# One written order for every engine: from units 0 to 8 to all 48 attention units

## The chip, the cores and the metric

The kernel runs on one core of a Trainium2 chip. Its time is the device time of one execution in microseconds; lower is better. The time before is given as the median of three runs.

## The reference

Three parts in a row, all with float32 inputs and outputs.

```python
# attention: q, k, v of [4, 8, 1152, 64]
q_pool = q.reshape(B, H, S // 2, 2, D).mean(axis=3)
scores = scale * np.matmul(q_pool, k.transpose(0, 1, 3, 2))
attn = softmax(scores)
x = matmul(attn, v)                  # heads beside each other: [2304, 512]
# first dense part
h = x @ w_in                         # [2304, 2048]
g = where(h >= 1, h, where(h <= -1, 0, (h + 1) ** 2 / 4))
x = g @ w_out                        # [2304, 512]
# second dense part
h = maximum(maximum(x @ w1, x @ w2), x @ w3)   # [2304, 768]
return h @ w_o2
```

The weights come as 64-bit numbers and are turned into float32 on the chip (`to_f32`).

## The kernel before

**Units.** The attention is cut into 48 units: unit `n` is batch `b = n // 12`, a block `i` of 192 pooled queries (three in a batch) and a pair of heads `p` (four). In each unit `soft` (L398) runs three times (`who` 0, 1, 2: head 0, head 1, and the 64 last queries of both): scores on PE into a tile of three PSUM banks (`sc`, L394), row maximum on DVE (L409), its scaling to the bias `nb` (L411 on DVE or L414 on ACT), exponential on ACT (L416). For batches 1 to 3 the weights are then split into two float16 halves: for `who` 0 and 1 by ACT and DVE into `hl` (L480, L481), which a transposing DMA on SP's queue carries into `pt` (L482); for `who` 2 by transposes on PE (`tr`, L458), and ACT and DVE write `pt` from PSUM (L466, L467). For batch 0 all three go by transposes on PE in float32. The tiles `sc` and `tr` take turns in two buffers of one pool. `shares` (L423) brings the row sums into the shape of `av`, by two transposes on PE (L433, L434) and two copies on ACT into `R`. `av` (L485) multiplies with v, and `rows` (L518) splits a block's result into the two halves `xh`.

**Dense steps.** For each block of 192 rows there are eight steps up (`up_step`, L550: 24 matmuls `ph`, then ACT `t2`, two DVE operations, ACT and DVE for the halves of `g`) and four steps down (`down_step`, L581: 48 matmuls `py`, two ACT operations, a store to `y_d`). `ph`, `py`, `av` and the small sums take turns in two PSUM banks.

**Weights and inputs.** w_in is loaded and converted in eight chunks (`w_in_chunk`, L191), w_out in eight chunks (`w_ou_chunk`, L234): ACT takes the absolute value (L167), DVE works four times (L169 to L175), ACT squares. Five of the eight chunks of w_out go through one raw buffer (`raw_ou`). When all eight are in, `w_ou_last` (L261) takes the largest value over the partitions, with one transpose on PE (`max_ou`, L113), and only then every chunk is scaled into its halves (L256, L258). k, v and q of later batches are loaded, normed, split (POOL at L280, DVE at L282) and, for k and q, transposed by DMA.

**What sets the order.** Each engine takes its instructions in the order in which they stand, and SP's queue issues the DMAs in its own. Inside `tc.manual_schedule(engines=...)` the named engines keep the order in which the program writes them; elsewhere a scheduler places each instruction. Before, PE is in written order over the whole attention, and the others only in `opening()`: the table `OPENING` there names one piece of work a word (`s01` is unit 0, `who` 1; `w`, `o` weight chunks; `u`, `y` dense steps up and down; `k`, `v`, `q` the inputs; `r` `shares`; `a` `av`; `x` `rows`), and each word takes that generator to its next `yield`. It ends with unit 8's work and with every weight chunk. Units 9 to 47 then run in a loop over `ORDER`: `s0` one score stage, `t0` what follows its exponential, `r` and `a1` `shares` and `av` of the unit before, `d` one call of the dense steps, `q` the next q. There PE's order is the written one, and ACT, DVE, POOL and SP go by the scheduler. After the attention (`at.close()`) the second dense part's weights are converted beside what is left of the dense steps, and its matmuls (`p`, L844) run to the end.

Of the kernel before, what the change touches and what calls it, by code (L numbers as in the profile page):

```python
# [19 lines left out]
K1 = (-2, 0, 2)  # L20
V1 = (1, 2, 3)
# [41 lines left out]
def body(ctx: ExitStack, tc: tile.TileContext, q, k, v, w_in, w_out, w1, w2, w3, w_o2, out):  # L63
# [246 lines left out]
    def k_steps(b, p):  # L310
# [30 lines left out]
    def q_steps(b, i, p):  # L341
# [56 lines left out]
    def soft(b, i, p, who):  # L398
# [14 lines left out]
        if not (FIRST(b, i, p) and who in NB_DVE):  # L413
            nc.scalar.activation(out=nb, in_=m, func=AF.Copy, scale=e, bias=PS)  # L414
# [8 lines left out]
    def shares(b, i, p):  # L423
# [8 lines left out]
        rs = R[b, i, p] if not FIRST(b, i, p) else psg.tile([P, 512], F32, tag="g1", name=f"rs{b}_{i}_{p}")  # L432
# [17 lines left out]
    def turned(b, i, p, who, pf):  # L450
        key = f"{b}_{i}_{p}_{who}"
        if who == 2 or WHOLE(b, p):
# [7 lines left out]
            if who == 2 and not FIRST(b, i, p):  # L460
# [17 lines left out]
        pt = new_pt(b, i, p)  # L478
# [103 lines left out]
    def down_step(b, i, m):  # L582
# [42 lines left out]
    events = {}  # L625

    def steps(gen, *counts):
        for c in counts:
            run(gen, c)
            yield  # L630

    for b in range(1, B):
        for p in range(NPAIR):
            t = 3 * (b * NBL * NPAIR - NPAIR + p + 1)
            for gen, at_ in ((steps(k_steps(b, p), 1, 1, -1), K1), (steps(v_steps(b, p), 1, 1, -1), V1)):
                for x in at_:
                    events.setdefault(t + x, []).append(gen)

    def now(t):
        for gen in events.get(t, ()):  # L640
            next(gen)

    behind = {}

    def piece(name):

        kind, num = name[0], name[1:]
        if kind == "q":
            return q_steps(*units[int(num)])
        if kind == "k":  # L650
            return k_steps(0, int(num))
        if kind == "v":
            return v_steps(0, int(num))
# [11 lines left out]
        if kind == "r":  # L665
            return shares(*units[int(num)])
# [278 lines left out]
```

## Time and profile before

| | us |
|---|---|
| median of the three runs | 1227.33 |
| the three runs | 1227.33, 1227.65, 1220.1 |
| the profiled execution, its own time | 1221.76 |
| its span, first to last instruction | 1220.0 |
| TensorE busy in the span | 1067.8 (88%) |
| VectorE busy | 844.4 (69%) |
| ScalarE busy | 743.4 (61%) |
| GpSimd busy | 143.0 (12%) |

The profile shows one execution. PE is TensorE's matmuls, PEld its weight loads, DVE VectorE, ACT ScalarE, POOL GpSimd, SP the queue that issues the DMAs. PEclk is the TensorE clock that was granted, 1.00 for full speed. The cuts between stages below are the starts of the first row maximum (DVE L409) of units 0, 8, 12, 15, 21, 27, 33, 39 and 47, and the first matmul of the second dense part.

### The profile page before, as it was taken

The numbers are of one execution on the slowest core, as the hardware profiler recorded it, in microseconds if no ns is written. First come the engines' busy times: TensorE is split into PE (matmuls) and PEld (weight loads), VectorE is DVE, ScalarE is ACT, GpSimd is POOL, SyncE is SP. The second block draws the span as 40 slices with busy tenths as digits, with TensorE's granted clock in tenths as the row PEclk, the third lists the DMA queues.
The fourth block names the chain that finished last, engine by engine and source line by source line (L and its number), as shares of the span: only waits on it lengthen the run. The fifth ranks groups of instructions, "written<-read, shape, count | busy, mean of one in ns | idle before, by whom it ended". The sixth has DMA issues, their size and how long they took to land. (4 is left out here: it accounts for less than half of the span.)

```text
span 1220.0 us, 26675 instructions
## 1 busy us (share of the span) xinstructions
PE 1067.8 (88%) x11061; PEld 873.8 (72%) x11061; DVE 844.4 (69%) x1431; ACT 743.4 (61%) x1310; POOL 143.0 (12%) x160
## 2 busy tenths in 40 slices
PE   2778827999999888999987999998978999999998
PEld 1556726787888677888776788887967776777774
DVE  5999957678878789887878878776888552422220
ACT  4988847777778667777867777776465311112111
POOL 3211110121101122010112100000301020100000
PEclk9799968999999899999999999999989999999999
DMA  9844332358666678556588655546443220000001
GB/s 303 233 131 151 87 127 53 91 130 165 111 109 111 133 166 192 103 115 109 104 171 178 119 98 98 99 85 157 143 130 126 73 68 18 10 27 18 18 18 45
DMA packets 273755, 134.92 MB, mean 111 GB/s; under 512 B 229088, under 2 KB 256736, under 8 KB 272608
## 3 DMA queue, kind: packets, MB, share of 16 engines
q1 hardware_dynamic: 273632, 133.20, 47.6%
q8 instruction: 87, 1.43, 0.5%
q14 instruction: 36, 0.29, 0.1%
HBM read 62.39 MB, written 9.44 MB: 59 GB/s over the span
## 5 line engine op out<-in xcount | busy, mean ns | idle before, releaser
L844 PE MATMUL p<-yh,wm 128*128 128x288 f16 x1728 | 216.2, 288 | 4.4 <-POOL yh L815 3.4
L409 DVE TENSOR_REDUCE st<-sc 128x1 f32<-128x1152 f32 x144 | 194.5, 1351 | 27.3 <-PE sc L394 26.9
L592 PE MATMUL py<-g,wou 128*128 128x192 f16 x2304 | 200.8, 248 | 13.2 <-ACT g L576 6.3
L567 PE MATMUL ph<-xh,win 128*128 128x192 f16 x2304 | 206.3, 247 | 2.4 <-DVE xf L514 1.6
L844 PEld LDWEIGHTS <-wm 128*128 128x128 f16 x1728 | 169.5, 98 | 50.8 <-issue 5.0
L592 PEld LDWEIGHTS <-wou 128*128 128x128 f16 x2304 | 192.3, 98 | 15.4 <-issue 10.0
L567 PEld LDWEIGHTS <-win 128*128 128x128 f16 x2304 | 191.2, 98 | 12.1 <-issue 10.4
L416 ACT ACTIVATE pf<-sc,st,esc 128x1152 f32<-128x1152 f32 x144 | 188.6, 1310 | 12.6 <-DVE st L411 5.8
L394 PE MATMUL sc<-kst,qst 128*64 128x512 f16 (+3 forms) x1152 | 171.3, 335 | 21.2 <-ACT pf L416 8.8
L394 PEld LDWEIGHTS <-qst 128*64 128x64 f16 (+1 forms) x1152 | 82.2, 106 | 80.7 <-issue 30.9
L458 PE MATMUL tr<-ident,pf 128*128 128x128 f32 x648 | 90.2, 290 | 18.6 <-ACT pf L416 18.3
L852 ACT ACTIVATE h<-mx 128x288 f16<-128x288 f32 x48 | 21.2, 442 | 130.4 <-DVE mx L850 130.4
L481 DVE TENSOR_TENSOR hl<-pf,hl 128x1152 f16<-128x1152 f32 x72 | 97.1, 1349 | 2.7 <-ACT hl L480 2.7
L500 PE MATMUL av<-pt,vhl 128*64 128x192 f16 x1944 | 94.3, 259 | 2.9 <-DMA pt<-hl 2.9
L458 PEld LDWEIGHTS tr<-ident,pf 128*128 128x128 f32 x648 | 76.4, 150 | 28.0 <-ACT pf L416 18.5
L500 PEld LDWEIGHTS <-vhl 128*64 128x64 f16 x1944 | 86.4, 117 | 13.6 <-issue 10.5
L849 DVE TENSOR_TENSOR mx<-p,mx 128x288 f32<-128x288 f32 x48 | 21.9, 455 | 106.0 <-PE p L844 105.5
L480 ACT ACTIVATE hl<-pf 128x1152 f16<-128x1152 f32 x72 | 83.5, 1159 | 0.9
L576 ACT ACTIVATE g<-t,dgs 128x384 f16<-128x384 f32 x96 | 58.6, 613 | 39.3 <-DVE t L574 39.0
L578 DVE SCALAR_TENSOR_TENSOR g<-t,dgs,g 128x384 f16<-128x384 f32 x96 | 66.4, 694 | 19.2 <-ACT g L576 18.8
L467 DVE TENSOR_TENSOR pt<-tr,pt 128x1152 f16<-128x1152 f32 x36 | 48.8, 1356 | 27.8 <-ACT pt L466 27.8
L573 DVE TENSOR_SCALAR t<-t 128x384 f32<-128x384 f32 x96 | 42.6, 444 | 32.5 <-ACT t L571 30.7
(178 smaller groups left out, 1282.8 us busy)
## 6 DMA issues: line engine op xcount, KB each, us to landing
vn<-in_v_dram SPq DMA_DIRECT2D x16, 576.0 KB, 4.0
kn<-in_k_dram SPq DMA_DIRECT2D x16, 576.0 KB, 4.4
raw_m<-in_moe_w_dram SPq DMA_DIRECT2D x12, 768.0 KB, 5.3
raw_in<-in_moe_w_in_dram SPq DMA_DIRECT2D x8, 1024.0 KB, 6.2
qn<-in_q_dram SPq DMA_DIRECT2D x24, 256.0 KB, 3.3
raw_ou<-in_moe_w_out_dram SPq DMA_DIRECT2D x10, 512.0 KB, 4.3
qst<-qst SPq DMA_DIRECT2D x48, 96.0 KB, 2.2
y_d<-ys SPq DMA_DIRECT2D x48, 96.0 KB, 1.8
```

Source lines behind the costliest of these rows:

```text
L394: nc.tensor.matmul(sc[m0:m1, n0:n1], qst[b, i, p][who][:, var, m0:m1], ks[:, h, n0:n1], start=(var == 0), stop=(var == 1))
L409: nc.vector.tensor_reduce(out=m, in_=sc, axis=AX.X, op=ALU.max, negate=True)
L416: nc.scalar.activation(out=pf, in_=sc, func=AF.Exp, bias=nb, scale=e, accum_out=sums[b, i, p][:, who:who + 1])
L458: nc.tensor.transpose(tr[:, c * P:(c + 1) * P], pf[:, c * P:(c + 1) * P], ident)
L480: nc.scalar.activation(out=hl[:, 0], in_=pf, func=AF.Copy)
L481: nc.vector.tensor_tensor(out=hl[:, 1], in0=pf, in1=hl[:, 0], op=ALU.subtract)
L500: nc.tensor.matmul(acc[64 * h:64 * h + 64], vhl[b, p][:, vi, h, c, :], pt[:, h, pi * KT + c, :], start=(c == 0 and e == 0), stop=(c == KT ...
L567: nc.tensor.matmul(ph[:, a], win[:, wi, kt, ff * P:(ff + 1) * P], x[:, xi, kt], start=(kt == 0 and e == 0), stop=(kt == KD - 1 and e == 2))
L576: nc.scalar.activation(out=g[:, 0, fs, :], in_=t2, func=AF.Copy, scale=gs)
L578: nc.vector.scalar_tensor_tensor(out=g[:, 1, fs, :], in0=t2, scalar=gs, in1=g[:, 0, fs, :], op0=ALU.mult, op1=ALU.subtract)
L592: nc.tensor.matmul(py, wou[:, ff // 2, wi, ff % 2, m * P:(m + 1) * P], g[:, gi, ff, :], start=(ff == 0 and e == 0), stop=(ff == NF - 1 and ...
L844: nc.tensor.matmul(ph[:, :NB2], wm[:, wi, i, kt, ff * P:(ff + 1) * P], yh[:, yi, kt, n0:n0 + NB2], start=(kt == 0 and e == 0), stop=(kt == ...
```

## The change

The loop over `ORDER`, the timed events for k and v, and `OPENING` are gone. One table, `ATTENTION`, names 2279 steps, and all five engines run in written order over the whole attention. It holds k, v and q of every batch, the conversion of w_in and w_out, all steps up and the steps down of the first eleven of the twelve blocks; the last block's four steps down stay with the scheduler. Four generators yield once or twice more, so that a step can stand between the ACT and the DVE half of a split (`turned`) and between the ACT operations and the store (`down_step`). The bias `nb` is made on DVE for all 12 units of batch 0 (before: units 0 to 8), and the same units have a PSUM bank of their own for `shares`.

```diff
-ORDER = {True: "s0 r d s1 d t0 a1 q t1 s2 d d t2",
-         False: "s0 t- d d r s1 t0 a1 s2 t1 q d d"}
-FROM = 9
-FIRST = lambda b, i, p: b == 0 and 4 * i + p < FROM
-NB_DVE = (0, 1, 2)
+NB_DVE = ((0, 1, 2), ())
+OWN_BANK = (True, False)
+ATTENTION = """
+w0 q0 w1 q2 v0 w0 v1 v2 q0 w0 v3 k0 q0 k1 w0 w1 q2 q0 w0 w3 w1 q0 q2 v0 w1 v0 v1 v1 q0 w1 w2 q2 q0 v0 v2 q2 w0
...
+EVERY = {mybir.EngineType.PE, mybir.EngineType.Activation, mybir.EngineType.DVE, mybir.EngineType.Pool,
+         mybir.EngineType.SP}
...
-        if FIRST(b, i, p) and who in NB_DVE:
+        if who in NB_DVE[b > 0]:
             nc.vector.tensor_scalar(out=nb, in0=m, scalar1=e, scalar2=PS, op0=ALU.mult, op1=ALU.add)
...
-        rs = R[b, i, p] if not FIRST(b, i, p) else psg.tile([P, 512], F32, tag="g1", name=f"rs{b}_{i}_{p}")
+        rs = R[b, i, p] if not OWN_BANK[b > 0] else psg.tile([P, 512], F32, tag="g1", name=f"rs{b}_{i}_{p}")
...
                 nc.scalar.activation(out=hi, in_=tr, func=AF.Copy)
+                yield
                 nc.vector.tensor_tensor(out=lo, in0=tr, in1=hi, op=ALU.subtract)
...
         nc.scalar.activation(out=hl[:, 0], in_=pf, func=AF.Copy)
+        yield
         nc.vector.tensor_tensor(out=hl[:, 1], in0=pf, in1=hl[:, 0], op=ALU.subtract)
+        yield
+        pt = new_pt(b, i, p)
         nc.sync.dma_start_transpose(out=pt[:, who, :, 0:P], in_=hl.rearrange("p a b -> p (a b)"))
...
         nc.scalar.activation(out=py, in_=py, func=AF.Square, scale=gd, accum_out=y2[:, b, i, m:m + 1])
+        yield
         copy_q.dma_start(out=y_d[b][:, m, i * NB:(i + 1) * NB], in_=ys)
...
-    order = tc.manual_schedule(engines=ORDERED)
-    order.__enter__()
-    with tc.manual_schedule(engines=OTHERS):
-        opening()
...
-    for n, (b, i, p) in list(enumerate(units))[FROM:]:
-        with tc.issue_after(issued["q"]) if n < LEAD else nullcontext():
-            for word in ORDER[WHOLE(b, p)].split():
-                attend(n, word)
...
+    gens = {}
+    with tc.manual_schedule(engines=EVERY):
+        for name in ATTENTION.split():
             if name not in gens:
                 gens[name] = piece(name)
             run(gens[name], 1)
```

**Place one, PE at the largest value of w_out.** Before, PE's row there (`tr0_2_0_2` is the last transpose of unit 8, `max_ou` the transpose that needs all chunks of w_out, `sc0_2_1_0` the first scores of unit 9):

```order
L567 MATMUL ph0_0_6_1621<-xh0_0_996,win_73 128x192
L458 MATMUL tr0_2_0_2_1660<-ident_80,pf0_2_0_2_1651 128x128 x9
L113 MATMUL max_ou_1695<-ident_80,um_ou_1689 128x128
L394 LDWEIGHTS qst0_2_0_1095
L394 MATMUL sc0_2_1_0_1720<-kst0_1_229,qst0_2_0_1095 128x512
```

Now, in the changed kernel (`sc0_2_1_2` is the last scores of unit 9, `av0_2_0` unit 8's product with v):

```order
L472 MATMUL sc0_2_1_2_1871<-kst0_1_245,qst0_2_0_1526 64x128
L191 MATMUL max_ou_1889<-ident_80,um_ou_1837 128x128
L576 MATMUL av0_2_0_1895<-pt_0_2_0_1700,vn0_0_138 64x192 x18
L184 MATMUL sum_k1_1_1925<-sqk1_1_1893,ones_78 128x1
L536 MATMUL tr0_2_1_1_1929<-ident_80,pf0_2_1_1_1922 128x128 x9
```

`max_ou` has moved from ahead of all three score stages of unit 9 to behind them.

**Place two, DVE at the same point.** Before, DVE's row up to the first row maximum of unit 9 (`wou`, `raw_ou` are chunks of w_out, `um_ou` their largest values):

```order
L170 TENSOR_SCALAR wou_74<-wou_74 128x1024
L173 SCALAR_TENSOR_TENSOR wou_74<-raw_ou_708,wou_74 128x1024
L175 SCALAR_TENSOR_TENSOR wou_74<-raw_ou_708,wou_74 128x1024
L169 TENSOR_SCALAR raw_ou_708<-raw_ou_708 128x1024
L170 TENSOR_SCALAR raw_ou_708<-raw_ou_708 128x1024
L173 SCALAR_TENSOR_TENSOR raw_ou_708<-raw_ou_708 128x1024
L175 SCALAR_TENSOR_TENSOR raw_ou_708<-raw_ou_708 128x1024
L265 TENSOR_REDUCE um_ou_1689<-mx_ou_853 128x1
...
L115 TENSOR_REDUCE U_ou_75<-max_ou_1695 128x1
...
L409 TENSOR_REDUCE st0_2_1_0_1730<-sc0_2_1_0_1720 128x1
```

Now (`st0_2_0_2` is unit 8's last row maximum, `st0_2_1_0` and `st0_2_1_1` are unit 9's first two):

```order
L247 TENSOR_SCALAR raw_ou_589<-raw_ou_589 128x1024
L248 TENSOR_SCALAR raw_ou_589<-raw_ou_589 128x1024
L487 TENSOR_REDUCE st0_2_0_2_1760<-sc0_2_0_2_1713 128x1
L489 TENSOR_SCALAR st0_2_0_2_1760<-st0_2_0_2_1760,esc0_2_0_1645 128x1
L251 SCALAR_TENSOR_TENSOR raw_ou_589<-raw_ou_589 128x1024
L253 SCALAR_TENSOR_TENSOR raw_ou_589<-raw_ou_589 128x1024
...
L487 TENSOR_REDUCE st0_2_1_0_1820<-sc0_2_1_0_1763 128x1
...
L343 TENSOR_REDUCE um_ou_1837<-mx_ou_695 128x1
...
L487 TENSOR_REDUCE st0_2_1_1_1884<-sc0_2_1_1_1860 128x1
```

The last two chunks stood in a row before unit 9; now the last chunk stands among unit 8's work, the one before it further ahead, and the largest value is taken inside unit 9.

**Place three, PE in a regular unit (42).** Before, what stands between the transposes of unit 41's last stage and the second scores of unit 42 (`ph3_0_2` is one step up, 24 pairs of a weight load and a matmul):

```order
L458 MATMUL tr3_1_1_2_10464<-ident_80,pf3_1_1_2_10342 128x128 x9
L567 LDWEIGHTS win_73
L567 MATMUL ph3_0_2_10476<-xh3_0_10075,win_73 128x192
...
L433 MATMUL tr3_1_1_2_10464<-ident_80,rb3_1_1_10509 128x128
L434 MATMUL tr3_1_1_2_10464<-ident_80,sm3_1_1_10193 128x128
L394 LDWEIGHTS qst3_1_2_10361
L394 MATMUL sc3_1_2_1_10516<-kst3_2_8600,qst3_1_2_10361 128x512
```

Now:

```order
L536 MATMUL tr3_1_1_2_10473<-ident_80,pf3_1_1_2_10451 128x128 x9
L648 LDWEIGHTS win_73
L648 MATMUL ph3_0_2_10490<-xh3_0_10195,win_73 128x192
...
L648 MATMUL ph3_0_3_10522<-xh3_0_10195,win_73 128x192
...
```

Behind the first step up now stands a second one (`ph3_0_3`), which before stood behind the third scores; the two transposes of `shares` stand behind the second scores.

## Rows read from the trace of the kernel before

**Rows 1.** Busy time by stage: us, busy (instructions) per engine, PEclk, DMA share, GB/s

```profile
0.00:30.60 30.60, 7.68 (x24) 4.37 (x24) 17.19 (x43) 14.50 (x23) 9.65 (x13) 1.00 0.98 303
30.60:148.90 118.30, 95.28 (x820) 72.38 (x822) 113.30 (x205) 103.91 (x152) 17.39 (x18) 0.93 0.53 150
148.90:255.10 106.20, 73.29 (x722) 61.30 (x723) 69.35 (x122) 68.95 (x113) 14.88 (x18) 0.86 0.35 94
255.10:304.00 48.90, 44.57 (x535) 38.46 (x536) 42.62 (x78) 37.45 (x71) 8.66 (x10) 1.00 0.77 157
304.00:396.90 92.90, 88.56 (x1116) 77.34 (x1115) 74.93 (x111) 72.66 (x134) 9.24 (x14) 1.00 0.63 110
396.90:506.90 110.00, 94.84 (x1125) 81.96 (x1124) 91.45 (x155) 79.02 (x146) 20.18 (x21) 0.95 0.74 156
...
599.70:710.10 110.40, 95.01 (x1126) 81.37 (x1124) 91.46 (x155) 78.76 (x146) 19.49 (x21) 0.95 0.73 146
710.10:833.50 123.40, 117.62 (x1483) 102.66 (x1482) 94.39 (x133) 93.75 (x170) 5.80 (x11) 1.00 0.53 94
833.50:929.90 96.40, 78.10 (x918) 74.78 (x917) 77.38 (x125) 57.62 (x93) 12.80 (x6) 0.93 0.45 138
929.90:1220.00 290.10, 284.38 (x2096) 201.92 (x2095) 97.38 (x206) 63.94 (x130) 15.75 (x15) 0.99 0.12 39
```

**Rows 2.** Timeline, 149 to 200 us: start, us, engine, line, operation, idle before

```profile
169.07 1.12 ACT L167 ACTIVATE wou<-raw_ou 128x1024 f32<-128x1024 f32 x1 [2.29 <-DMA raw_ou<-in_moe_w_out_dram]
170.23 0.69 DVE L169 TENSOR_SCALAR wou<-wou 128x1024 f32<-128x1024 f32 x1 [2.79 <-ACT wou L167]
...
173.69 1.22 DVE L175 SCALAR_TENSOR_TENSOR wou<-raw_ou,wou 128x1024 uint32<-128x1024 uint32 x1
...
179.81 1.12 ACT L167 ACTIVATE raw_ou<-raw_ou 128x1024 f32<-128x1024 f32 x1 [3.65 <-DMA raw_ou<-in_moe_w_out_dram]
...
186.77 0.48 PE L113 MATMUL max_ou<-ident,um_ou 128*128 128x128 f32 x1 [22.55 <-DVE um_ou L100]
```

**Rows 3.** Timeline of unit 42, 756 to 771 us

```profile
756.15 1.15 PE L458 MATMUL tr<-ident,pf 128*128 128x128 f32 x9
...
757.14 2.14 PE L567 MATMUL ph<-xh,win 128*128 128x192 f16 x24
757.34 1.13 ACT L466 ACTIVATE pt<-tr 128x1152 f16<-128x1152 f32 x1 [1.14 <-PE tr L458]
...
758.50 1.36 DVE L467 TENSOR_TENSOR pt<-tr,pt 128x1152 f16<-128x1152 f32 x1 [0.79 <-ACT pt L466]
758.74 1.31 ACT L416 ACTIVATE pf<-sc,st,esc 128x1152 f32<-128x1152 f32 x1
...
760.00 0.30 PE L433 MATMUL tr<-ident,rb 128*128 128x128 f32 x1 [0.72 <-DVE pt L467]
...
760.25 1.14 PE L394 MATMUL sc<-kst,qst 128*128 128x512 f16 x6
...
760.65 0.36 DVE L573 TENSOR_SCALAR t<-t 128x384 f32<-128x384 f32 x1 [0.79 <-ACT t L571]
761.04 0.56 DVE L574 SCALAR_TENSOR_TENSOR t<-t 128x384 f32<-128x384 f32 x1
...
761.32 2.42 PE L500 MATMUL av<-pt,vhl 128*64 128x192 f16 x54
...
764.05 0.61 DVE L578 SCALAR_TENSOR_TENSOR g<-t,dgs,g 128x384 f16<-128x384 f32 x1
764.16 6.05 SPq L482 DMA_TRANSPOSE pt<-hl  x2
...
766.63 4.12 PE L592 MATMUL py<-g,wou 128*128 128x192 f16 x48
```

**Rows 4.** Timeline, 25 to 29 us: POOL and DVE beside each other

```profile
25.54 2.05 POOL L280 TENSOR_SCALAR kpre<-kn,sb 128x1152 f16<-128x1152 f32 x1 [1.16 <-issue]
...
26.54 2.13 DVE L175 SCALAR_TENSOR_TENSOR wou<-raw_in,wou 128x1024 uint32<-128x1024 uint32 x1
```

More of the change, by code (lines that the diff above doesn't have):

```diff
@@ L1 @@
-from contextlib import ExitStack, nullcontext
+from contextlib import ExitStack
 import concourse.bass as bass
@@ L459, in turned @@
             yield
-            if who == 2 and not FIRST(b, i, p):
+            if who == 2 and not OWN_BANK[b > 0]:
                 R[b, i, p] = rs
@@ L639, in now @@
[L639 to L643, printed above, removed]
     def piece(name):
         kind, num = name[0], name[1:]
[L648 to L653, printed above, removed]
-        if kind == "w":
-            return w_in_last() if num == "i" else w_in_chunk(int(num))
-        if kind == "o":
-            return w_ou_last() if num == "o" else w_ou_chunk(int(num))
-        if kind in "uy":
-            i, m = int(num[0]), int(num[1])
-            begun.add((kind, 0, i, m))
-            return (up_step if kind == "u" else down_step)(0, i, m)
-        if kind == "s":
-            n, who = int(num[:-1]), int(num[-1])
-            return soft(*units[n], who)
-        if kind == "r":
-            return shares(*units[int(num)])
-        if kind == "a":
-            return av(*units[int(num)])
-        if kind == "x":
-            return rows(0, int(num))
@@ L672, in opening @@
-    def opening():
-        gens = {}
-        for name in OPENING.split():
+        if name == "wi":
+            return w_in_last()
+        if name == "oo":
+            return w_ou_last()
+        if kind in "suy":
+            n, m = (int(x) for x in num.split("."))
+            if kind == "s":
+                return soft(*units[n], m)
+            begun.add((kind, *divmod(n, NBL), m))
+            return (up_step if kind == "u" else down_step)(*divmod(n, NBL), m)
+        n = int(num)
+        if kind in "kv":
+            return (k_steps if kind == "k" else v_steps)(*divmod(n, NPAIR))
@@ L676, in opening @@
+        if kind in "wo":
+            return (w_in_chunk if kind == "w" else w_ou_chunk)(n)
+        if kind == "x":
+            return rows(*divmod(n, NBL))
+        return {"q": q_steps, "r": shares, "a": av}[kind](*units[n])
+    gens = {}
+    with tc.manual_schedule(engines=EVERY):
+        for name in ATTENTION.split():
             if name not in gens:
@@ L678, in opening @@
             run(gens[name], 1)
-        for name in gens:
-            run(gens[name])
-    order = tc.manual_schedule(engines=ORDERED)
-    order.__enter__()
-    with tc.manual_schedule(engines=OTHERS):
-        opening()
-    for t in range(3 * FROM):
-        now(t)
-    def attend(n, word):
-        b, i, p = units[n]
-        kind, num = word[0], word[1:]
-        if kind == "s":
-            who = int(num)
-            behind[n, who] = soft(b, i, p, who)
-            run(behind[n, who], 3)
-            now(3 * n + who)
-        elif kind == "t":
-            key = (n - 1, 2) if num == "-" else (n, int(num))
-            if key in behind:
-                run(behind.pop(key))
-        elif kind == "r":
-            run(shares(*units[n - 1]))
-        elif kind == "a":
-            attended(n - int(num))
-        elif kind == "d":
-            next(dense, None)
-        elif kind == "q":
-            if n % 2 == 1 and n + 1 < len(units):
-                run(q_steps(*units[n + 1]))
-    def attended(n):
-        b, i, p = units[n]
-        run(av(b, i, p))
-        if p == NPAIR - 1:
-            run(rows(b, i))
-    for n, (b, i, p) in list(enumerate(units))[FROM:]:
-        with tc.issue_after(issued["q"]) if n < LEAD else nullcontext():
-            for word in ORDER[WHOLE(b, p)].split():
-                attend(n, word)
-    last = len(units)
-    run(behind.pop((last - 1, 2)))
-    run(shares(*units[last - 1]))
-    for n in range(last - DEPTH, last):
-        attended(n)
-    order.__exit__(None, None, None)
+    for gen in gens.values():
+        assert next(gen, "end") == "end"
     at.close()
```

141 lines of the change are left out of this document (103 added, 38 removed).

## The prediction

> **What bounds the kernel now.** I read busy time by stage first, cut at the first row maximum of chosen units, then the timeline where a stage was too long, then a regular unit. [rows 1] shows five kinds of stage. From 30.6 to 148.9 us (units 0 to 7) DVE is busy 113.3 of 118.3: there the written order of all engines already stands, and the busiest engine is 96% full. From 148.9 to 255.1 (units 8 to 11) no engine reaches 73.3 of 106.2. The regular stages take 92.9 us for six units and 123.4 for eight, 15.43 a unit, with PE busy 117.62 of 123.4. The two long ones at 396.9 and 599.7 take 110 for six units, where k and v of the next batch are prepared: PE 94.84, DVE 91.45. The tail from 833.5 to 929.9 has PE at 78.1 and DVE at 77.38 of 96.4. From 929.9 PE is busy 284.38 of 290.1, and nothing there is changed: I carry 290.1 over.
>
> In the slow stage the rows to see are [rows 2]: PE stands 22.55 us before `max_ou`. It is next in PE's row, and needs the last chunk of w_out. The chunks come one by one through one raw buffer: from one chunk's first ACT operation (169.07) to the next one's (179.81) is 10.74 us, while DVE works some 4 us on each (two operations of 0.69 and two of 1.22). All engines stand on this chain, with unit 9 ready behind it.
>
> In a regular unit [rows 3] PE runs the transposes `tr`, one step up (757.14 and 2.14 long, so to about 759.2), and then stands until 760.00 for DVE's `pt`; the second scores start at 760.25, and the exponential that frees their buffer ends at 758.74 + 1.31 = 760.05. That is PE's idle time of (123.4 - 117.62) / 8 = 0.72 us a unit.
>
> **The change, stage by stage.** The sum goes by the profiled execution: 1221.76, of which 1220.0 is its span, 1.8 around it.
>
> *Start.* SP now loads two chunks of w_in (128 x 2048 words of four bytes, 1.05 MB each) and one more q (0.39 MB) ahead of the first k: 2.5 MB, at the 303 GB/s of [rows 1] 8.2 us later. DVE has 10 us more to do ahead of the first row maximum (two chunks more at 3.8, and the halves of two at 1.3), but can begin earlier. Bounds 0 and +11; I take +6: 36.6.
>
> *Units 0 to 7.* DVE's work is the same to within 1 us, and was 96% full. Four chunks of w_out now lie in units 5 to 8, each with about 10.5 us of DVE work from one to the next, just under the chain's 10.74. I add 0.75 for each: 118.3 + 3 = 121.3. Bounds: 113 (DVE alone) and 140 (if each chunk cost 5 us).
>
> *Units 8 to 11.* Two chunk conversions go ahead of unit 8; steps up fall from 9 to 2 in matmuls, from 9 to 3 and 4 in their DVE work; steps down from 3 to 1. DVE, by [rows 2, 3]: 69.35 - 6 x (0.36 + 0.56) - 5 x 0.61 - 2 x 3.8, less one split of k and two of q (2.6), plus nine biases moved from ACT (1.9): 52. ACT falls by the same pieces, 68.95 to about 55. PE: 73.29 - 7 x 2.14 - 2 x 4.12 = 50. `max_ou` now stands behind unit 9's three score stages, and the largest value is taken inside that unit, so the 22.55 has unit 9 and k of batch 1 as cover; if that cover is late, it comes back. With ACT at 55 and DVE at 52, both well filled but neither alone, I take 90% of the busier: 62. Bounds 55 and 85 (106.2 less the work that left DVE, if no wait goes).
>
> *Regular units* (15 to 20, 27 to 32, 39 to 46: 20). Two steps up now stand between `tr` and the second scores: 4.2 us of PE work from 757.14, against 2.9 until the exponential ends and 2.7 until `pt` is written. DVE now does a `g` half and sometimes a q split ahead of `pt`, 1.2 us, and the transposes that wait for it stand behind the second scores, so there is room. Late next is nothing: ACT has 93.75 / 8 = 11.7 and DVE 11.8 a unit. Between 0 and 0.72 I take 0.57, as some gaps are the pipeline's own: 14.86 a unit. Stages: 92.9 - 3.4 = 89.5; 92.8 (506.9 to 599.7) - 3.4 = 89.4; 123.4 - 4.6 = 118.8.
>
> *Units 12 to 14.* Equal work, PE busy 44.57 of 48.9: I take 46, between the two.
>
> *Long stages* (21 to 26, 33 to 38). What was put off is made up here: two steps up and one down in each, 2 x 2.14 + 4.12 = 8.4 us of PE work, 3.1 of DVE. PE 94.84 + 8.4 = 103.2, DVE 94.5. Lower bound 103, upper 110 + 8.4 = 118.4 (if the extra work is simply added). Written order held DVE at 96% in the opening, so I take PE at 97%: 106 and 106.4.
>
> *Tail.* Ahead of unit 47 as many dense steps are done as before (84 up, 38 down). Behind the last `av` stand 8 up and 8 down, before 10 and 9: 2 x 2.14 + 4.12 = 8.4 us less on PE, moved into unit 47. DVE's work is unchanged at 77. The scheduler still places the conversion of the last weights. I take 92, between 88 (all of it) and 97.
>
> Sum: 36.6 + 121.3 + 62 + (46 + 89.5 + 106 + 89.4 + 106.4 + 118.8) + 92 + 290.1 = 1158.1; with 1.8 around it 1159.9. The median of the three runs is 5.6 above the profiled one, and one of the three 1.7 below it; I add 2 and say 1162.
>
> **The rivals.**
>
> *The put-off work is only late (no better pace behind unit 12).* For it: PE's row in a regular unit hardly differs, and 95% is already high. Against: the 0.72 has a named cause that the new row removes. From 255.1 to 833.5 are 578.4 us; with the 16.8 us of dense work added, 595.2 instead of 556.1: 1201.
>
> *The chain of chunks stays the bound.* Five chunks through one buffer cost at least 10.74 each whatever the order. If DVE's work between them doesn't fit and each of the four in units 5 to 8 costs 5 us more: +20, 1182. For it: all engines now wait in written order, so one late chunk holds them all. Against: 10.5 beside 10.74.
>
> *POOL and DVE hold each other up.* [rows 4] shows DVE's L175 at 2.13 us beside a POOL operation of 2.05; alone it took 1.22 [rows 2]. If in the long stages every POOL microsecond stops DVE, they cannot be shorter than 94.5 + 20.18 = 114.7: +17 on both, 1179. Against: 91.45 already holds the collisions of before. The Trainium skill, SBUF — State Buffer, section "SBUF: two separate sides", says why: the port pair that the two share is an exclusive lock, held for a whole instruction, so that the other is blocked. The row agrees for this one pair of operations.
>
> *SP's written queue comes late, and the kernel is slower.* Place: the two transposing DMAs of each unit of batches 1 to 3 (36 units). They take 6.05 us to issue [rows 3], now in fixed order with the loads of q, k and v; `av` waits for them. Laid out with the durations of [rows 3] (an estimate), the second `hl` is ready some 14.3 us into a unit, and `av` starts 7.5 into the next, 8 us later. One issue takes 3, landing some 2 more, so about 3.4 are spare. Lateness beyond 3.4 costs PE one for one. At 6 us late: 36 x 2.6 = 94, so 1256. It decides the sign from about 5.2 us (36 x 1.8 = 65, all of the gain). Against: the regular stages of before show no such wait at `av`, with DMA share 0.53 to 0.63.
>
> *Everything fits.* Start and units 0 to 7 lose nothing (-9), units 8 to 11 take 56, the long stages 103, the tail 88: -25, 1137.
>
> **Chances.** Forecast 0.50, no better pace 0.17, chunks 0.11, ports 0.07, SP's queue 0.05, everything fits 0.10. The range 1136 to 1203 takes in all but the slower case and some of the edges. The forecast alone: 1148 to 1174. A measurement of this kernel can tell about 1% from no change: faster by more 0.89, within 0.05, slower 0.06.
>
> **What would show it.** Right: PE's wait before `max_ou` under 5 us; unit 12's first row maximum near 220; 14.9 us from unit to unit in regular stages, with no PE wait on the exponential; the long stages at 106 with PE over 100 busy; the second dense part's first matmul near 868. Wrong: regular units still at 15.4; `av` waiting for `pt<-hl`; unit 8 later than 165; a tail of 97 or more, which would mean that the last weights' conversion bounds it, and not PE.

## The result, and the profile after

The changed kernel takes 1155.88 us (median of four, 1153.67 to 1159.74), the kernel before in the same comparison 1226.52: a ratio of 0.944, 95% interval 0.940 to 0.948. Its profiled execution took 1153.67, with a span of 1151.9 against 1220.0.

Busy time by stage of the changed kernel, with the columns of [rows 1]; the cuts are again the first row maximum (now DVE L487) of units 0, 8, 12, 15, 21, 27, 33, 39 and 47 and the first matmul of the second dense part (now L854):

```profile
0.00:39.80 39.80, 7.67 (x24) 4.45 (x24) 29.81 (x57) 21.22 (x32) 11.48 (x14) 1.00 1.00 314
39.80:163.30 123.50, 100.79 (x892) 77.62 (x892) 115.75 (x202) 102.59 (x151) 18.41 (x19) 0.93 0.52 139
163.30:223.90 60.60, 51.20 (x439) 39.01 (x439) 51.99 (x93) 49.35 (x76) 10.74 (x10) 0.89 0.32 83
223.90:272.30 48.40, 45.46 (x504) 38.39 (x503) 42.85 (x68) 39.43 (x72) 11.71 (x11) 1.00 0.72 154
272.30:361.90 89.60, 89.60 (x1167) 79.33 (x1164) 79.33 (x124) 72.86 (x134) 10.45 (x15) 1.00 0.70 130
361.90:462.10 100.20, 98.50 (x1232) 87.52 (x1231) 90.24 (x152) 82.50 (x156) 22.36 (x21) 1.00 0.87 172
462.10:548.80 86.70, 86.70 (x1111) 76.63 (x1109) 76.20 (x119) 72.43 (x135) 9.85 (x14) 1.00 0.63 118
548.80:653.90 105.10, 99.14 (x1220) 87.59 (x1218) 91.00 (x153) 82.46 (x155) 20.62 (x21) 0.98 0.79 154
653.90:770.00 116.10, 116.10 (x1483) 102.63 (x1482) 98.53 (x155) 93.80 (x174) 7.49 (x15) 1.00 0.60 105
770.00:862.90 92.90, 78.19 (x919) 75.22 (x918) 77.45 (x123) 55.54 (x87) 11.09 (x6) 0.91 0.49 146
862.90:1151.90 289.00, 282.95 (x2096) 201.56 (x2095) 98.27 (x208) 65.68 (x137) 15.27 (x15) 1.00 0.12 40
```

Read it against [rows 1] by PE's idle time, the stage less PE's busy time. Over the span it fell from 152.2 to 95.6, and PE's busy time from 1067.8 to 1056.3; together these are the 68.1 us. The idle time went in units 8 to 11 (32.9 to 9.4), in the two long stages (15.2 to 1.7 and 15.4 to 6.0) and in the regular units (39 to 46: 5.8 to 0). It grew in the start, 22.9 to 32.1, and is about as before in units 0 to 7, 23.0 to 22.7. One count in the table misleads: one `av` (50 of its 54 matmuls, 2.2 us) now falls behind the cut at 272.3, so units 15 to 20 hold 51 matmuls more than before (1167 against 1116), and units 12 to 14 lack them.

A regular unit of the changed kernel (42), PE alone; it answers to [rows 3]. No row has an idle time in brackets, and from one `tr` to the next are 14.5 us:

```profile
697.21 1.15 PE L536 MATMUL tr<-ident,pf 128*128 128x128 f32 x9
698.20 4.12 PE L648 MATMUL ph<-xh,win 128*128 128x192 f16 x48
702.16 1.14 PE L472 MATMUL sc<-kst,qst 128*128 128x512 f16 x6
703.14 0.28 PE L511 MATMUL tr<-ident,rb 128*128 128x128 f32 x1
...
711.72 0.50 PE L536 MATMUL tr<-ident,pf 128*128 128x128 f32 x3
```

At the largest value of w_out, where [rows 2] show 22.55 us, PE now comes straight from unit 9's scores:

```profile
181.31 1.17 PE L472 MATMUL sc<-kst,qst 128*64 128x512 f16 x12 [0.24 <-ACT pt L551]
182.41 0.32 PE L191 MATMUL max_ou<-ident,um_ou 128*128 128x128 f32 x1
182.66 3.15 PE L576 MATMUL av<-pt,vn 128*64 128x192 f32 x36
```

### The profile page after: what moved, and what is told of

It is laid out like the page before. It is cut to its first block, busy times and chain, and to the rows that moved or that the text cites. A ratio compares the mean times of both kernels' runs of the same rounds, so it can differ in the third digit from the quotient of the medians.

```text
span 1151.9 us, 26593 instructions
## 1 busy us (share of the span) xinstructions
PE 1056.3 (92%) x11061; PEld 870.0 (76%) x11061; DVE 851.4 (74%) x1440; ACT 737.9 (64%) x1301; POOL 149.5 (13%) x160
## 4 chain that ended last, share of the span: by engine, by line
PE 44%; DVE 3%; DMA 1%; ACT 1%; issue 1%; SPq 0%; POOL 0%; ACTq 0%; POOLq 0%; DVEq 0%
PE p L854 18%; PE py L673 7%; PE ph L648 6%; PE po L871 5%; PE sc L472 3%; PE av L581 3%; PE tr L536 1%; PE por L885 1%; DVE t L654 1%; DMA vn<-in_v_dram 0%; DVE st_m L247 0%; DMA raw_o<-in_moe_w_out_dram 0%; DVE st_m L253 0%; DVE st_m L251 0%; DMA kn<-in_k_dram 0%
## 5 line engine op out<-in xcount | busy, mean ns | idle before, releaser
L648 PE MATMUL ph<-xh,win 128*128 128x192 f16 x2304 | 209.0, 251 | 9.7 <-POOL xh L358 7.1
L854 PE MATMUL p<-yh,wm 128*128 128x288 f16 x1728 | 214.8, 286 | 1.6 <-DVE yh L827 0.8
L487 DVE TENSOR_REDUCE st<-sc 128x1 f32<-128x1152 f32 x144 | 194.7, 1352 | 20.9 <-PE sc L472 20.3
L648 PEld LDWEIGHTS <-win 128*128 128x128 f16 x2304 | 197.8, 100 | 14.3 <-issue 9.9
L854 PEld LDWEIGHTS <-wm 128*128 128x128 f16 x1728 | 169.0, 98 | 47.0 <-issue 2.5
L673 PEld LDWEIGHTS <-wou 128*128 128x128 f16 x2304 | 189.7, 98 | 13.8 <-issue 12.7
L859 DVE TENSOR_TENSOR mx<-p,mx 128x288 f32<-128x288 f32 x48 | 21.8, 456 | 105.1 <-PE p L854 104.6
L581 PE MATMUL av<-pt,vhl 128*64 128x192 f16 x1944 | 87.1, 247 | 0.0
L581 PEld LDWEIGHTS <-vhl 128*64 128x64 f16 x1944 | 79.3, 110 | 6.8 <-issue 6.4
L652 ACT ACTIVATE t<-ph,Uv 128x384 f32<-128x384 f32 x96 | 55.0, 574 | 15.7 <-PE ph L648 14.7
L871 PE MATMUL po<-wo,h 128*128 128x512 f16 x288 | 64.3, 379 | 0.0
L659 DVE SCALAR_TENSOR_TENSOR g<-t,dgs,g 128x384 f16<-128x384 f32 x96 | 62.0, 648 | 2.7 <-ACT g L657 2.4
```

The lines of the kernel that those rows point to most:

```text
L487: nc.vector.tensor_reduce(out=m, in_=sc, axis=AX.X, op=ALU.max, negate=True)
L581: nc.tensor.matmul(acc[64 * h:64 * h + 64], vhl[b, p][:, vi, h, c, :], pt[:, h, pi * KT + c, :], start=(c == 0 and e == 0), stop=(c == KT ...
L648: nc.tensor.matmul(ph[:, a], win[:, wi, kt, ff * P:(ff + 1) * P], x[:, xi, kt], start=(kt == 0 and e == 0), stop=(kt == KD - 1 and e == 2))
L659: nc.vector.scalar_tensor_tensor(out=g[:, 1, fs, :], in0=t2, scalar=gs, in1=g[:, 0, fs, :], op0=ALU.mult, op1=ALU.subtract)
L673: nc.tensor.matmul(py, wou[:, ff // 2, wi, ff % 2, m * P:(m + 1) * P], g[:, gi, ff, :], start=(ff == 0 and e == 0), stop=(ff == NF - 1 and ...
L854: nc.tensor.matmul(ph[:, :NB2], wm[:, wi, i, kt, ff * P:(ff + 1) * P], yh[:, yi, kt, n0:n0 + NB2], start=(kt == 0 and e == 0), stop=(kt == ...
```

## The experiments

Stage times below are one profiled execution of each kernel, cut as above. The same stage of kernels that share its order differs by up to 2.7 us from one profile to the next (units 0 to 7: 122.7 to 125.3; units 33 to 38: 104.5 to 107.2), and no less is read as a difference unless a wait shows it. Line numbers in some of these kernels are three lower than in the changed one.

### PE's row alone

`e1_phase` is the kernel before with one call of the dense steps more in unit 15. One turn in four is empty, so from there on each `d` of `ORDER` meets another step:

```diff
         for word in ORDER[WHOLE(b, p)].split():
...
+            if n == 15:
+                next(dense, None)
```

> The kernel before with one more turn of the dense steps consumed in unit 15, so that PE's row of a regular unit becomes: first scores, tr, step up, step up, shares, second scores, as in the changed kernel; the other engines stay with the scheduler. Theory A (PE's row alone removes the idle time of 0.72 us a unit): a regular unit takes 14.5 to 14.9 us instead of 15.4, the 20 regular units together 11 to 18 us less, the median 1208 to 1216. Rival B (the gain needs all engines in written order, or comes from work put off): a regular unit stays within 0.15 of 15.4 and the median within 4 us of before.

Measured: 1187.74 against 1224.41, ratio 0.970 (0.968 to 0.973). Its stages of units 15 to 20, 21 to 26 and 39 to 46:

```profile
308.30:395.50 87.20, 87.20 (x1112) 77.03 (x1111) 72.61 (x106) 69.40 (x131) 7.53 (x12) 1.00 0.61 110
395.50:499.50 104.00, 93.33 (x1128) 82.26 (x1127) 88.99 (x158) 79.07 (x150) 19.66 (x23) 0.97 0.82 167
...
691.50:808.20 116.70, 116.14 (x1483) 102.70 (x1481) 94.10 (x133) 91.03 (x170) 5.08 (x12) 1.00 0.61 99
```

Theory A holds for the regular units: they take 14.5 to 14.7 us with the other four engines still under the scheduler, and all 20 together 16.9 less, inside the 11 to 18 expected. The whole gain, 36.7 us, is over twice that. I had left out that the long stages have the same place in their units: they fell from 110 to 104, 12.6 together, without any written order of DVE, and the tail by 4.4. (The profiled execution is the slowest of its four, so the two profiles differ by 29.7 and not by 36.7.)

`e2_back` undoes the same thing in the changed kernel: the five words of the second step up of units 39 to 46 go back behind the third scores (here `u9.1` in unit 41; its first word is PE's, and `s41.1` and `s41.2` are the second and third scores):

```diff
-... s41.0 s40.2 u9.1 u9.0 r40 u8.7 u9.0 r40 s41.1 s41.0 u8.7 r40 a40 s41.1 u9.0 r40 u9.1 s41.0 s41.1 s41.2 a40 ...
+... s41.0 s40.2 u9.0 r40 u9.0 r40 s41.1 s41.0 r40 a40 s41.1 u9.0 r40 s41.0 s41.1 s41.2 u9.1 a40 ...
```

> The changed kernel with the second step up of units 39 to 46 moved back behind the third scores, all else in its written order. Theory A (what stands between tr and the second scores sets a regular unit): units 39 to 46 go from 14.5 to 15.2 to 15.4 us each, the stage from 116.1 to 121 to 124, with PE waiting for DVE's pt or the exponential. Rival B (the written order of the other engines gives the pace): 14.5 to 14.7 each, the stage at 116 to 118.

The eight units take 127.1 us (659.9 to 787.0), 15.9 each, above theory A's 15.4. PE waits again ahead of the second scores, now for the exponential (ACT L491), 7.6 us in seven waits over the stage; here one of them:

```profile
722.84 1.15 PE L533 MATMUL tr<-ident,pf 128*128 128x128 f32 x9
723.83 2.14 PE L645 MATMUL ph<-xh,win 128*128 128x192 f16 x24
726.89 1.14 PE L469 MATMUL sc<-kst,qst 128*128 128x512 f16 x6 [0.92 <-ACT pf L491]
```

The two runs show the cause from both sides: two steps up between `tr` and the second scores cover DVE's `pt` and the exponential, one doesn't. In the whole kernel the 1176.64 (one run) is 20.8 above the changed one; of that 11.0 lie in these units. The rest, 2.7 of it in the tail, lies in stages whose order is the same, and is not explained.

### Units 8 to 11: cover, put-off work, or the other engines' order

Five kernels take this stage apart. `e3_unit9` writes unit 9's score stages ahead of the largest value in `OPENING` of the kernel before (`FROM` becomes 10, which also gives unit 9 its bias on DVE and its `shares` a bank of their own; the four dense turns of unit 9 are made up in units 10 and 11):

```diff
-... o5 o6 s82 u06 s82 u06 u06 o6 o6 o6 o7 o6 o7 o7 o7 o7 oo oo oo ...
+... o5 o6 s82 u06 q10 s82 u06 u06 s90 r8 s91 s90 r8 o6 s91 r8 s90 q10 o6 s91 r8 s90 a8 o6 q10 s91 s92 s90
+a8 q10 o7 s91 q10 s92 o6 q10 s92 o7 q10 s92 o7 s92 q10 o7 o7 oo oo oo ...
```

> The kernel before with the three score stages of unit 9, and shares and av of unit 8 and the next q, put ahead of the largest value of w_out in the written table; the two stretches of scheduled units behind are unchanged. Theory A (the 22.55 us lacked cover): PE's wait before max_ou falls below 8 us and the median by 15 to 20, to 1207 to 1212. Rival B (the gain of units 8 to 11 in the changed kernel comes from dense steps and inputs put off, or the chunk chain bounds anyway): the wait or its like stays, the median within 8 us of before.

`e3c_put_off` takes the dense turns out of units 9 to 11 of the kernel before (`if n >= 12:` ahead of `next(dense, None)`), and `e3b_both` does both.

> The kernel before with the twelve turns of dense steps of units 9 to 11 put off to later units and nothing else: unit 9 still stands behind the largest value of w_out. Theory A (both are needed): PE's wait before max_ou stays at 18 to 24 us and unit 12's first row maximum at 241 to 255. Rival B (putting off alone is the gain of these units): unit 12 at 225 to 237.

> The kernel before with unit 9's score stages ahead of the largest value of w_out (as in the run e3_unit9) and, beside it, the twelve turns of dense steps of units 9 to 11 put off to later units; DVE, ACT, POOL and SP stay with the scheduler from unit 10 on. Theory A (cover and put-off dense steps are needed together, and no written order of the other engines): no wait at max_ou or for the scaled chunks of w_out above 6 us, units 8 to 11 take 76 to 88 us, unit 12's first row maximum at 225 to 237 (before 255.1, changed kernel 223.9). Rival B (the other engines' written order is what is needed): unit 12 stays behind 245.

`e7_pe_only` is the changed kernel with PE alone in written order from `s9.0` on:

```diff
-    with tc.manual_schedule(engines=EVERY):
-        for name in ATTENTION.split():
+    cut = names.index("s9.0")
+    with tc.manual_schedule(engines={mybir.EngineType.PE}):
+        with tc.manual_schedule(engines=EVERY - {mybir.EngineType.PE}):
+            written(names[:cut])
+        written(names[cut:])
```

> The changed kernel with the whole table as PE's order, but from unit 9's first scores on ScalarE, VectorE, GpSimd and SP go by the scheduler, as before. Theory A (PE's row carries the gain behind unit 14, the written order of the others and of SP's loads carries that of units 9 to 11): regular units at 14.5 to 14.7 us, the two long stages 100 to 106, but units 8 to 11 take 70 us or more (60.6 in the changed kernel), so that unit 12's first row maximum is at 233 or later; in all 8 to 25 us slower than the changed kernel. Rival B (PE's row is all of it): unit 12 within 4 us of 223.9, the time within 5 us of 1155.9. Rival C (the others' written order is needed everywhere): regular units at 15.2 or more.

`e9_no_cover` is the changed kernel with the eight words `s9.0 s9.0 s9.0 s9.0 s9.1 s9.0 s9.2 s9.1` moved from ahead of the last `oo` to behind it.

> The changed kernel with the eight steps of unit 9 that stand ahead of the largest value of w_out moved behind it, on all engines. Theory A (these steps are the cover of the wait): PE waits 8 to 16 us before max_ou instead of not at all, and unit 12's first row maximum comes 6 to 14 us later, at 230 to 238. Rival B (the last chunks came early enough by themselves): the wait stays below 4 us and unit 12 within 3 us of 223.9.

| kernel | units 8 to 11 | PE busy there | wait at `max_ou` | unit 12 starts | time, us |
|---|---|---|---|---|---|
| before | 106.2 | 73.29 | 22.55 | 255.1 | 1226.52 |
| `e3c_put_off` | 99.0 | 55.19 | 23.53 | 250.4 | 1231.43 |
| `e3_unit9` | 119.1 | 82.97 | 4.98 | 268.2 | 1229.39 |
| `e3b_both` | 93.3 | 55.62 | 4.63 | 241.4 | 1224.69 |
| `e7_pe_only` | 70.8 | 52.40 | none | 234.1 | 1186.71 |
| `e9_no_cover` | 70.3 | 53.74 | 1.88 | 234.5 | 1166.97 |
| changed | 60.6 | 51.20 | none | 223.9 | 1155.88 |

The times are medians; those of the kernels from `e3c_put_off` to `e9_no_cover`, `e3_unit9` apart, are of one run each. The times of `e3c_put_off` and `e3b_both` don't price the stage, since their put-off turns are made up in the tail, which grows from 96.4 to 110.2 and 112.1. The ratio of `e3_unit9` (ten runs) is 1.005 (1.003 to 1.007), half a per cent slower. This kernel took the wait away as theory A said, and the time came back at once. (Its 82.97 us of PE are for 724 matmuls, before 722, at a granted clock of 0.81 and not 0.86.) PE's row there has a step down close behind `max_ou`, and its matmuls wait chunk by chunk for the scaled w_out; then the second k of batch 1 is late:

```profile
190.01 0.47 PE L113 MATMUL max_ou<-ident,um_ou 128*128 128x128 f32 x1 [4.98 <-DVE um_ou L100]
...
204.98 0.34 PE L592 MATMUL py<-g,wou 128*128 128x192 f16 x2 [1.10 <-ACT wou L256]
206.84 0.50 PE L592 MATMUL py<-g,wou 128*128 128x192 f16 x4 [1.51 <-DVE wou L258]
...
236.85 0.59 PE L106 MATMUL sum_k<-sqk,ones 128*128 128x1 f32 x2 [10.44 <-ACT kpre L297]
```

With the dense turns put off as well the waits for scaled chunks are gone, but the late k stays, in `e3b_both`:

```profile
187.48 0.47 PE L113 MATMUL max_ou<-ident,um_ou 128*128 128x128 f32 x1 [4.63 <-DVE um_ou L100]
...
220.25 0.59 PE L106 MATMUL sum_k<-sqk,ones 128*128 128x1 f32 x2 [13.00 <-ACT kpre L297]
```

So 241.4 lies between theory A's 237 and rival B's 245, and neither stands as put. Putting work off alone left the 22.55 in place (23.53), as theory A said. In the changed kernel the table loads both k's ahead of unit 8 and keeps `y0.0` behind unit 11's scores; the early k's were not tried by themselves. `e7_pe_only` keeps that PE row and takes away the others' written order from unit 9 on: 10.2 us come back here. `e9_no_cover` returns 9.7, with unit 12 at 234.5 as expected, but not as a long wait at `max_ou`, as I had put it; from unit 8's first row maximum to unit 9's are 24.9 us instead of 12.2, and PE's idle time in the stage grows from 9.4 to 16.6 in several waits.

`e7_pe_only` also splits the whole gain. Its span is 1184.8, so 35.2 of the 68.1 us are there with PE's row and the written part up to unit 8; 32.9 need the other engines' order. Its stages of units 8 to 11, 15 to 20, 21 to 26, 33 to 38 and 39 to 46:

```profile
163.30:234.10 70.80, 52.40 (x446) 39.09 (x444) 51.47 (x103) 52.39 (x82) 14.29 (x15) 0.88 0.38 93
287.10:377.10 90.00, 89.82 (x1167) 79.38 (x1166) 75.11 (x113) 70.56 (x135) 8.90 (x14) 1.00 0.62 114
377.10:489.30 112.20, 101.46 (x1235) 89.77 (x1233) 91.97 (x164) 82.12 (x156) 19.09 (x22) 0.98 0.75 156
575.40:687.40 112.00, 100.35 (x1226) 87.96 (x1225) 95.10 (x164) 81.46 (x157) 22.90 (x22) 0.98 0.72 145
687.40:803.10 115.70, 115.70 (x1479) 102.23 (x1478) 94.02 (x134) 91.28 (x172) 5.31 (x12) 1.00 0.60 101
```

The regular units need PE's row alone. The long stages don't: with the dense work made up in them they take 112 under the scheduler and 100.2 and 105.1 in written order. I had expected 100 to 106 there, and the time is 30.8 above the changed kernel's, not 8 to 25.

### The start

`e4_start` puts the first words, up to `s2.0`, back into the order of `OPENING`.

> The changed kernel with its first steps, up to the first scores of unit 2, in the order of the kernel before (k ahead of most of w_in), the rest in its own order. Theory A (the later first row maximum is only VectorE work done early): unit 0's first row maximum goes back from 39.8 to about 31, and that of unit 8 stays within 3 us of 163.3. Rival B (the later first unit is time lost): unit 8's comes 5 to 9 us earlier, at 154 to 158, and the end with it.

```profile
0.00:31.10 31.10, 7.68 (x24) 4.38 (x24) 17.20 (x43) 14.40 (x23) 9.80 (x13) 1.00 0.98 300
31.10:168.80 137.70, 101.58 (x885) 79.23 (x886) 126.12 (x215) 109.64 (x158) 19.84 (x20) 0.91 0.52 148
```

Unit 0 starts at 31.1 again, and unit 8 not earlier but 5.5 us later, at 168.8: theory A's 3 us are missed too, and rival B falls. The whole run takes 1157.89 (one run). From the kernel before to the changed one, unit 8 is later by the DVE work done ahead of it: DVE is busy 130.5 of 148.9 before and 145.6 of 163.3 in the changed kernel, so that 18.4 and 17.7 are left idle. In `e4_start` almost the same work, 143.3, leaves 25.5 idle. The lateness is there by unit 2, whose first row maximum comes at 75.0 and not at 69.1, with DVE idle for 18.8 us up to there against 10.7; from unit 2 to unit 8 the two are alike (93.8 and 94.2). So the late first unit is not time lost: DVE does work there that it otherwise does later, with more idle time.

### What is left: the tail and a late v

Two edits tried the tail, where PE still idles 14.7 us. `e5_tail` moves `y10.0` and `y10.1` ahead of `u11.0` on PE, `e6_no_pool` takes GpSimd out of the split of w1 to w3:

```diff
-... a47 r47 y9.3 a47 x11 x11 x11 u11.0 u11.1 ...
+... a47 y10.0 r47 y9.3 a47 y10.1 y10.0 x11 x11 x11 y10.0 y10.1 u11.0 u11.1 ...
```

```diff
-            if kt == 0:
-                nc.scalar.activation(out=wm[:, 0, :, kt, :], in_=st, func=AF.Copy, scale=s[:, kt:kt + 1])
-                nc.gpsimd.tensor_scalar(...)
-                nc.gpsimd.tensor_tensor(...)
-            else:
-                split_rows(...)
+            split_rows(...)
```

> The changed kernel with two of the last-but-one block's steps down (8.2 us of PE work) moved in PE's row ahead of the last block's steps up, into the 7.1 and 1.4 us in which PE waits for xh behind the last av. Theory A (the tail is bound by PE's row): the tail from unit 47's first row maximum to the second dense part's first matmul goes from 92.9 to 85 to 89 us, the median from 1155.9 to 1148 to 1152. Rival B (the tail is bound by the conversion of the last weights on VectorE and ScalarE): the tail stays within 2 us of 92.9.

> The changed kernel with the split of the first of the four blocks of w1 to w3 done as the other three are (ScalarE, then one VectorE operation) and not on GpSimd. In the changed kernel a VectorE operation that alone takes 0.35 us took 4.69 beside GpSimd's 4.73 and one of 0.56 took 2.47, and TensorE then waited 5.73. Theory A (GpSimd's two operations stop VectorE): VectorE does 2 to 2.6 us more but loses 6 less, TensorE's wait of 5.73 falls below 2.5, the tail of 92.9 falls by 2 to 5 us. Rival B (the tail hangs on the loads or on ScalarE, and the stop is hidden): the tail within 1.5 us of 92.9 or longer.

The changed kernel's tail, all engines, shows why both were worth a run:

```profile
802.04 0.32 PE L648 MATMUL ph<-xh,win 128*128 128x192 f16 x1 [7.10 <-POOL xh L358]
...
812.67 4.73 POOL L775 TENSOR_TENSOR wm<-st_m,wm 128x2304 f16<-128x2304 f32 x1
812.92 4.69 DVE L654 TENSOR_SCALAR t<-t 128x384 f32<-128x384 f32 x1
...
820.12 0.80 PE L673 MATMUL py<-g,wou 128*128 128x192 f16 x4 [5.73 <-ACT g L657]
```

`e5_tail`: tail 91.4, median 1156.35 (ratio 0.944, 0.939 to 0.949). `e6_no_pool`: tail 91.9, median 1160.12 (0.946, 0.943 to 0.950). Rival B holds both times. The waits that were aimed at went and others came: in `e5_tail` the 7.10 is 0.62, and PE waits 3.81 and 4.33 later; in `e6_no_pool` the 5.73 is 2.00, followed by 2.58.

`e8_three` joins both edits with an earlier load of v.

> The changed kernel with three edits together: the two steps down ahead of the last block's steps up (run e5_tail), no GpSimd in the split of w1 to w3 (run e6_no_pool), and v of pair 3 of batch 3 loaded some 8 us earlier, ahead of a q load on SP's queue (the changed kernel's ScalarE waits 5.49 for it and TensorE 3.75). Theory A (the first two each only moved the tail's bound to the other): the tail falls from 92.9 to 85 to 89 us and units 33 to 38 from 105.1 to 101 to 103, the median to 1146 to 1151. Rival B (the tail has a third bound, the loads of the last weights): the tail stays at 91 to 93, the median 1152 to 1156, all from the earlier v.

Measured: 1168.49, ratio 0.955 (0.953 to 0.957), 12.6 above the changed kernel, which neither theory had. The tail is 93.2, so the two edits give nothing together either, and what bounds it stays open: DVE's row there is the scheduler's, and no run rewrote it. The load was my mistake. I moved v of pair 3, and the one that ScalarE waits for is that of pair 2. Moved up, it took the raw buffer that the k behind it needs, and units 33 to 38 grew to 114.2. ACT stood 8.97 for that k and PE 5.39 behind it:

```profile
597.24 1.16 ACT L372 ACTIVATE kpre<-kn 128x1152 bf16<-128x1152 f32 x1 [8.97 <-DMA kn<-in_k_dram]
...
600.17 4.16 PE L469 MATMUL sc<-kst,qst 128*64 128x512 f16 x18 [5.39 <-ACT pf L491]
```

`e10_v` is the changed kernel with the right word moved:

```diff
-... s36.0 y6.2 v15 r35 q42 ... s37.0 s36.2 u7.6 v14 u7.7 ...
+... s36.0 y6.2 v15 v14 r35 q42 ... s37.0 s36.2 u7.6 u7.7 ...
```

> The changed kernel with one load moved on SP's queue: v of pair 2 of batch 3 (issued at 616.43 there, ScalarE waits 5.49 for it and TensorE 3.75) now stands ahead of the q load issued at 608.13, where the raw buffer that it takes, that of v of pair 3, comes free at 607.75. Theory A (this load's place in the queue is what is left of the wait): ScalarE's wait falls below 1.5, TensorE's below 1, units 33 to 38 from 105.1 to 101 to 103, the median 1151 to 1154. Rival B (what stands behind it, the q load and the transposes, is late instead, as in the run e8_three): the stage stays within 1 us of 105.1 or grows.

In the changed kernel, SP, ACT and PE at this load:

```profile
616.43 0.54 SPq L369 DMA_DIRECT2D vn<-in_v_dram  x1
...
621.97 1.16 ACT L375 ACTIVATE vhl<-vn 128x1152 bf16<-128x1152 f32 x1 [5.49 <-DMA vn<-in_v_dram]
...
623.27 0.38 PE L184 MATMUL sum_v<-sqv,ones 128*128 128x1 f32 x2 [3.75 <-ACT vhl L375]
```

In `e10_v` the load goes out 7.5 us earlier, ACT doesn't wait, and the stage takes 101.4:

```profile
608.97 0.37 SPq L366 DMA_DIRECT2D vn<-in_v_dram  x1
...
617.36 1.15 ACT L372 ACTIVATE vhl<-vn 128x1152 bf16<-128x1152 f32 x1
```

```profile
549.60:651.00 101.40, 97.40 (x1219) 86.09 (x1217) 90.83 (x152) 82.57 (x154) 21.12 (x21) 1.00 0.79 160
```

Theory A holds in the stage: 3.7 us, and the 101.4 lies below the six kernels that have this load in its old place and all engines in written order (104.5 to 107.2). The median is 1154.05, the ratio to the kernel before 0.943 (0.940 to 0.945). That is 1.8 below the changed kernel, and the intervals overlap, so the whole time doesn't tell the two apart.

## Why the prediction was right

The forecast was 1162 in a range of 1136 to 1203; 1155.88 was measured. Against the profiled execution (1159.9 forecast, 1153.67 measured) the sum is 6.2 too high, and the stages add up to it. The two causes that it named, no cover at `max_ou` and one step up too few ahead of the second scores, are among those that the runs show; several terms were mis-sized, and some of their errors offset each other.

**Start and units 0 to 7**: 36.6 and 121.3 forecast, 39.8 and 123.5 measured. The +6 was the term mis-sized: the stage grew by 9.2, since DVE had 12.6 us more to do there (29.81 against 17.19), where I had counted 10, and used only 3.4 of its idle time for it. A chunk of w_in costs DVE 4.8 us in the start (four operations of 0.68, 1.09, 1.79 and 1.22 in the mean), and not 3.8. "DVE's work is the same to within 1 us" for units 0 to 7 was off too, 115.75 against 113.30. The stage grew by 5.2, 2.45 of it DVE's extra work. The 2.75 left are near the 3 that I had put on four chunks; that their chain causes them was not tried.

**Units 8 to 11**: 62 forecast, 60.6 measured, with DVE at 51.99 (52 forecast), PE at 51.20 (50) and ACT at 49.35 (55). That the sum came so near is in part luck: ACT was over 5 too high, and the busier engine filled 86% of the stage, not 90%. No wait stands at `max_ou`. The reason given, unit 9 as cover, was half of it: `e3_unit9` shows that cover alone is paid back by a step down that waits for scaled chunks and by a late k, and `e7_pe_only` that 10 us hang on the other engines' order.

**Units 12 to 14**: 46 forecast, 48.4 measured. Of the 2.9 us that I took off for equal work only 0.5 came, although one `av` left the stage. Why was not tried.

**Regular units**: 14.86 forecast, 14.5 measured (units 27 to 32 and 39 to 46). The cause was right and shown from both sides (`e1_phase`, `e2_back`). "Some gaps are the pipeline's own" was the wrong step: all of the 0.72 went, and PE's busy time fell by another 0.19 a unit (117.62 to 116.10 over eight). Most of that lies in the steps up, which now stand in pairs: 4.12 us for two, against 2.14 for each. Nothing new came late, as I had said. Units 15 to 20 came out at 89.6 beside a forecast of 89.5, but that is luck: they hold the 2.2 us of the `av` that moved over the cut.

**Long stages**: 106 and 106.4 forecast, 100.2 and 105.1 measured, the first below my lower bound of 103, and PE was busy 98.50 and 99.14, not over 100. I had added 8.4 us to PE's 94.84, and that number held matmuls at a lower clock: [rows 1] gives 0.95 granted there, the changed kernel's row 1.00. The 0.95 is a mean: in the kernel before the clock was at half of the full speed (1.2 of 2.4 GHz) from 419.4 to 426.3 and from 443.4 to 446.8, and each time PE was in a long wait or 1.2 us behind one, of 3.35 and 3.92 us. Here are the first of the two and both waits; the `av` takes 4.14 us there, and 2.42 at full speed [rows 3]:

```profile
419.40:426.30 6.90, 5.61 (x52) 4.25 (x53) 4.07 (x5) 5.51 (x10) 0.00 (x0) 0.51 0.38 106
420.69 2.08 PE L394 MATMUL sc<-kst,qst 128*128 128x512 f16 x6 [3.35 <-ACT pf L416]
422.70 4.14 PE L500 MATMUL av<-pt,vhl 128*64 128x192 f16 x54
...
442.17 0.30 PE L433 MATMUL tr<-ident,rb 128*128 128x128 f32 x1 [3.92 <-DVE pt L467]
```

At 0.95 of the time, 94.84 is 90.1, and with 8.4 this is 98.5, which is what PE was busy; that it fits to the digit is chance, since the cuts move some matmuls. In the first long stage the matmuls of `av` show it, before and after (in units 39 to 46 of the kernel before, at 1.00, they take 247 ns too):

```profile
L500 PE MATMUL av<-pt,vhl 128*64 128x192 f16 x324 | 17.6, 276 | 0.0
```

```profile
L581 PE MATMUL av<-pt,vhl 128*64 128x192 f16 x324 | 14.5, 247 | 0.0
```

The second one keeps 6.0 us of idle time, 3.75 of it the late v of `e10_v`.

**Tail**: 92 forecast, 92.9 measured. With 8.4 us of PE work moved ahead of the last `av` the tail fell by 3.5; in `e1_phase`, where only 2.1 us (one step up) moved so, it fell by 4.4, so that this work is the cause isn't shown. That this bound isn't PE alone I had named as a sign, at 97 or more; the edits of the tail show it already at 93. The second dense part, carried over at 290.1, took 289.0.

**The rivals.** Work only put off: no, the regular units run 6% faster. The chain of chunks: units 0 to 7 took 2.2 more than forecast, not 20. SP's queue: in units 39 to 46 PE has no wait at all, `av` included. POOL and DVE: the first long stage would have had to take 94.5 + 20.18, or 112.6 with the busy times that were measured (90.24 and 22.36); it took 100.2. Some pairs of operations there leave each other alone, and some don't. DVE's `pt` beside POOL's `kpre` takes 1.36 us as in [rows 3]; DVE's `t` beside POOL's `qn` takes 1.15 where [rows 3] have 0.36:

```profile
363.83 1.22 POOL L358 TENSOR_SCALAR kpre<-kn,sb 128x1152 f16<-128x1152 f32 x1 [5.62 <-DVE sm L504]
364.02 1.36 DVE L546 TENSOR_TENSOR pt<-tr,pt 128x1152 f16<-128x1152 f32 x1
...
458.55 2.85 POOL L433 TENSOR_TENSOR qn<-qn 128x384 f32<-128x384 f32 x2 [8.64 <-DMA qn<-in_q_dram]
459.39 1.15 DVE L654 TENSOR_SCALAR t<-t 128x384 f32<-128x384 f32 x1
```

The Trainium skill, SBUF — State Buffer, section "SBUF: two separate sides", calls the shared port pair an exclusive lock, with conditions on the operations. The tail agrees for one pair of operations (4.69 beside 4.73), and the first rows above show a pair that it doesn't bind; the lifted stop in `e6_no_pool` brought no time.

## What to carry to other kernels

Look at what stands on the busiest engine between a producer and the wait for it: here one step up more at one place, got by two lines that shift the phase, gave half of what a table of 2279 steps gave. The written order of the other engines paid where several streams meet (loads, conversion, made-up dense work), not in the steady part. A wait covered at one place can return at the next thing that was late behind it, and a load moved up on a queue can take a buffer from another; so move one thing, and read the stage again. A bound from busy time must be taken at the clock that the stage will have without its waits.

## What was not expected of the hardware

The granted clock of a stage is part of its price: in units 21 to 26 it went from 0.95 to 1.00 when the waits of 3.35 and 3.92 us by its two slow stretches went, and PE's time for the same work fell with it by 4.7 us (94.84 to 90.1, which is the 98.50 measured less the 8.4 added). In the tail a GpSimd operation of 4.73 us on two inputs held a VectorE operation of 0.35 us for 4.69.
